# Attention bursts spaced one to a chunk, and a weight conversion with its own tiles, in a fused attention and cosine-FFN kernel

## The chip, the cores and the metric

The kernel runs on one core of one Trainium2 chip. The metric is the device time of one execution in microseconds (us). Three executions of the kernel before took 988.85, 989.06 and 987.37 us, so the median is 988.85 us. The profile was taken of a further execution, of 985.93 us.

## The reference, cut to what matters

```python
# batch 8, heads 8, sequence 576, head size 64; 4608 tokens, model size 512, hidden size 2048
scores = matmul(q, k.T) / 8
mask_local   = (0 <= i - j) & (i - j < 32)            # heads 0 to 3
mask_strided = (0 <= i - j) & (i % 32 == j % 32)      # heads 4 to 7
attn = softmax(where(mask, scores, -1e9))             # denominators + 1e-9
x    = matmul(attn, v)             # to 4608 x 512, heads side by side
h    = x @ w_in                    # 512 x 2048
out  = (h * cos(h)) @ w_out        # 2048 x 512
```

Everything is in 32-bit floats at the kernel's borders. Eight batches of 576 tokens make 4608 tokens.

## The kernel before, in words

**The feed-forward part.** Tokens are handled in 12 blocks of 384 (TB). For block j and for each of 16 slices f of the hidden size (128 rows each) there is one *chunk* (j, f). `hidden` makes h in one PSUM bank from 12 matmuls. The operands are split into a rounded part and a remainder: x_hi and x_lo, wi_h and wi_l, and three products of them are summed for each of four slices of the model size. Then h * cos(h) is made by a chain over two engines: ScalarE rounds h to a multiple of the period (line 377), VectorE subtracts it (378), ScalarE takes the sine shifted by a quarter (381), VectorE multiplies by h (384). Only after line 384 is the bank of h free; there are two such banks (`ps_h`, bufs=2). ScalarE then rounds the result to g_hi (387), and GpSimd makes the remainder g_lo (388). `outer` multiplies g by the slice of w_out with nine matmuls into three accumulators. `outer` runs three chunks behind `hidden` (LAG = 3).

**The attention part.** Each batch has ten *units*: four strided ones, then six local ones (two head pairs for each of three stretches of 192 tokens). A unit makes scores on TensorE, a softmax over VectorE, ScalarE and GpSimd, transposes on TensorE, products with v on TensorE, and a copy and a DMA of the result to a DRAM tensor xT. `load_x(j)` reads the four slices of a block back from xT: a DMA into x_raw, a cast to x_hi on VectorE (361) and a remainder x_lo on GpSimd (362).

**The three stages.** First, the 20 units of batches 0 and 1 run alone (0 to about 61 us). Second, blocks 0 and 1 run together: chunk (0, f), then chunk (1, f-1), while the weights of slice f are loaded and converted, and then three chunks of block 2. Third comes the steady loop: blocks 2 to 11, chunk by chunk, with the units of batches 2 to 7 put between the chunks in *bursts*. It numbers its chunks n from 3 to 159, where n = 16 (j - 2) + f. Burst k issues the transposes of unit k-2, the products of unit k-3 and the scores of unit k. At which chunk burst k is issued comes from linear interpolation between the pairs of KNOTS (chunk, burst), cut to whole chunks. In this loop TensorE's order is written out by hand (`in_turn`: each matmul after the one before it).

**The weights.** They come as 64-bit floats, seen as pairs of 32-bit words (low, top). `load_weight` takes one block of 128 x 512 numbers (512 KB): a DMA on SP's queue into the tile `raw`, of which the pool `cv` keeps two; on VectorE a shift of the low words (line 120) and an or with the sign of the top words (123); on ScalarE a scaling of the top words in place (128); on VectorE a last shift and or (129), whose result stands in the low words of the same tile; on ScalarE the cast to the rounded weights (133); on GpSimd the remainder (134). So a landing tile is in use until line 134 has read it. For each f, one such block of w_in and one of w_out are converted. The first operation of each (120) is ordered behind line 378 of the chunk two slices before (`after`, AHEAD = 2).

**What sets the order.** Each engine, and SP's queue of DMAs, works in the order of its instructions. Apart from TensorE in the steady loop, a scheduler chooses that order from the program's order and from its own estimate of the times. An operation that it expects to be ready early is moved forward, and blocks what is behind it if its input is late on the chip.

**Lines that the prediction names**: 118 (DMA of a weight block), 120, 123, 128, 129, 133, 134 (its conversion), 210 to 231 (softmax), 254 and 297 (scores), 264 and 313 (transposes), 273 and 327 (products), 279 and 281 (copy and store of a local unit), 360 to 362 (`load_x`), 371 to 388 (`hidden`), 395 (`outer`).

## Time and profile before

| what | value |
|---|---|
| median of three executions | 988.85 us |
| profiled execution: whole time | 985.93 us |
| profiled execution: span of the core's instructions | 984.1 us |
| granted TensorE clock, mean | 0.997 |
| TensorE (PE) busy | 954.8 us, 97% |
| VectorE (DVE), ScalarE (ACT), GpSimd (POOL) busy | 48%, 51%, 39% |
| bytes moved by DMA | 80.14 MB |

The engines are called PE, PEld (the loading of PE's weights, beside its matmuls), DVE, ACT, POOL and SP. A row of a timeline has the start in us from the span's start, the duration in us, the engine, the line, the operation, out<-in and the shape; in brackets the idle time before it and what ended it. "SPq" and "ACTq" are the instructions that issue DMAs. A row of groups has the count, the busy time, the mean in ns, and the idle time just before them. The row of a stretch has the stretch, its length, each engine's busy time with its number of instructions, the granted clock, the DMA engines' share and GB/s.

### The profile page before, as it was taken

The numbers are of one execution on the slowest core, as the hardware profiler recorded it, in microseconds if no ns is written. First come the engines' busy times: TensorE is split into PE (matmuls) and PEld (weight loads), VectorE is DVE, ScalarE is ACT, GpSimd is POOL, SyncE is SP. The second block draws the span as 40 slices with busy tenths as digits, with TensorE's granted clock in tenths as the row PEclk, the third lists the DMA queues.
The fourth block names the chain that finished last, engine by engine and source line by source line (L and its number), as shares of the span: only waits on it lengthen the run. The fifth ranks groups of instructions, "written<-read, shape, count | busy, mean of one in ns | idle before, by whom it ended". The sixth has DMA issues, their size and how long they took to land.

```text
span 984.1 us, 17763 instructions
## 1 busy us (share of the span) xinstructions
PE 954.8 (97%) x6890; PEld 833.9 (85%) x6890; DVE 467.9 (48%) x1005; ACT 499.6 (51%) x1043; POOL 384.4 (39%) x418
## 2 busy tenths in 40 slices
PE   9889899897999999999999999999999999999998
PEld 5678777786888888889888888888888888889997
DVE  6867777645454444444444444444444444222222
ACT  3665555555555545555445545555455544433433
POOL 2555544544344344334333343433333343232221
PEclk9999999999999999999999999999999999999999
DMA  8963333232332222112221332211221320100000
GB/s 247 296 216 108 108 111 124 66 108 73 104 87 91 68 87 79 43 51 75 69 59 43 110 85 75 75 51 54 90 60 35 111 60 14 46 15 1 33 1 32
DMA packets 48228, 80.14 MB, mean 81 GB/s; under 512 B 5904, under 2 KB 33296, under 8 KB 48144
## 3 DMA queue, kind: packets, MB, share of 16 engines
q1 hardware_dynamic: 38208, 69.35, 22.8%
q10 hardware_dynamic: 9936, 9.65, 2.8%
q8 instruction: 54, 0.88, 0.4%
q14 instruction: 30, 0.25, 0.1%
HBM read 60.11 MB, written 18.87 MB: 80 GB/s over the span
## 4 chain that ended last, share of the span: by engine, by line
PE 77%; DMA 2%; DVE 2%; ACT 2%; issue 1%; POOL 1%; POOLq 0%; DVEq 0%; ACTq 0%; SPq 0%
PE h L371 35%; PE acc L395 34%; PE acc L273 2%; PE acc L254 2%; DMA raw<-in_w_out 1%; PE acc L297 1%; PE acc L264 1%; PE acc L327 1%; PE acc L313 1%; DVE raw L120 1%; DVE raw L129 0%; ACT raw L128 0%; DVE r L378 0%; POOL g_lo L388 0%; DMA xT<-x_t 0%
## 5 line engine op out<-in xcount | busy, mean ns | idle before, releaser
L388 POOL TENSOR_TENSOR g_lo<-r,g_hi 128x384 fp32r<-128x384 f32 x192 | 198.6, 1034 | 401.1 <-issue 257.4
L371 PE MATMUL h<-x_hi,wi_h 128*128 128x384 f32 x768 | 267.1, 348 | 14.6 <-DVE r L384 14.6
L371 PE MATMUL h<-x_hi,wi_l 128*128 128x384 f32 x768 | 259.3, 338 | 0.0
L371 PE MATMUL h<-x_lo,wi_h 128*128 128x384 f32 x768 | 258.8, 337 | 0.0
L378 DVE SCALAR_TENSOR_TENSOR r<-r,h 128x384 f32<-128x384 int32 x192 | 106.2, 553 | 265.8 <-ACT r L377 247.3
L395 PE MATMUL acc<-wo_l,g_hi 128*128 128x512 f32 x576 | 227.4, 395 | 0.0
L395 PE MATMUL acc<-wo_h,g_lo 128*128 128x512 f32 x576 | 224.7, 395 | 0.0
L395 PE MATMUL acc<-wo_h,g_hi 128*128 128x512 f32 x576 | 224.0, 389 | 0.0
L371 PEld LDWEIGHTS h<-x_hi,wi_h 128*128 128x128 f32 x768 | 144.7, 188 | 31.5 <-DVE r L384 21.6
L381 ACT ACTIVATE r<-r,quarter 128x384 f32<-128x384 f32 x192 | 118.5, 617 | 91.1 <-DVE r L378 90.5
L371 PEld LDWEIGHTS h<-x_lo,wi_h 128*128 128x128 f32 x768 | 144.7, 188 | 5.0
L377 ACT ACTIVATE r<-h 128x384 int32<-128x384 f32 x192 | 93.4, 486 | 108.8 <-PE h L371 102.7
L384 DVE TENSOR_TENSOR r<-r,h 128x384 f32<-128x384 f32 x192 | 106.0, 552 | 81.8 <-ACT r L381 81.0
L371 PEld LDWEIGHTS h<-x_hi,wi_l 128*128 128x128 f32 x768 | 144.5, 188 | 0.3 <-POOL wi_l L134 0.3
L387 ACT CAST g_hi<-r 128x384 fp32r<-128x384 f32 x192 | 98.5, 513 | 83.5 <-DVE r L384 83.4
L395 PEld LDWEIGHTS acc<-wo_h,g_lo 128*128 128x128 f32 x576 | 108.0, 188 | 23.0
L395 PEld LDWEIGHTS acc<-wo_l,g_hi 128*128 128x128 f32 x576 | 108.0, 188 | 18.2
L395 PEld LDWEIGHTS acc<-wo_h,g_hi 128*128 128x128 f32 x576 | 108.2, 188 | 17.2
L362 POOL TENSOR_TENSOR x_lo<-x_raw,x_hi 128x384 fp32r<-128x384 f32 x48 | 50.0, 1042 | 107.1 <-DVE x_hi L361 86.8
L220 ACT ACTIVATE e_sb<-t_sb,shift 128x288 f32<-128x288 f32 (+1 forms) x60 | 32.9, 549 | 87.2 <-POOL t_sb L212 87.0
L361 DVE CAST x_hi<-x_raw 128x384 fp32r<-128x384 f32 x48 | 21.3, 445 | 53.0 <-DMA x_raw<-xT 50.7
L212 POOL TENSOR_TENSOR t_sb<-t_sb,mx 128x288 f32<-128x288 f32 (+1 forms) x60 | 41.8, 696 | 10.1 <-DVE mx L211 8.5
(66 smaller groups left out, 860.5 us busy)
## 6 DMA issues: line engine op xcount, KB each, us to landing
qk<-in_qkvs SPq DMA_DIRECT2D x32, 324.0 KB, 3.7
qk<-in_qkl SPq DMA_DIRECT2D x48, 208.0 KB, 2.7
x_raw<-xT SPq DMA_DIRECT2D x48, 192.0 KB, 2.4
out<-o SPq DMA_DIRECT2D x36, 256.0 KB, 2.1
raw<-in_w_in SPq DMA_DIRECT2D x16, 512.0 KB, 3.6
raw<-in_w_out SPq DMA_DIRECT2D x16, 512.0 KB, 3.7
v<-in_vl SPq DMA_DIRECT2D x48, 144.0 KB, 2.7
xT<-x_t ACTq DMA_DIRECT2D x16, 288.0 KB, 3.2
```

The costliest lines, as they stand in the source:

```text
L212: nc.gpsimd.tensor_tensor(out=t, in0=t, in1=mx[:, :n].unsqueeze(2).broadcast_to([P, n, w]), op=ALU.subtract)
L220: nc.scalar.activation(out=e, in_=t, func=AF.Silu, bias=shift1, scale=0.0625)
L361: nc.vector.tensor_copy(out=hi, in_=raw)
L362: nc.gpsimd.tensor_tensor(out=lo, in0=raw, in1=hi.bitcast(F32), op=ALU.subtract)
L371: mm = nc.tensor.matmul(h, w[:, f, c], x[c], start=(i == 0), stop=(i == len(ops) - 1))
L377: nc.scalar.activation(out=k, in_=h, func=AF.Copy, scale=1.0 / (2.0 * math.pi), bias=0.25)
L378: red = nc.vector.scalar_tensor_tensor(out=r, in0=k, scalar=-2.0 * math.pi, in1=h, op0=ALU.mult, op1=ALU.add)
L381: sin = nc.scalar.activation(out=r, in_=r, func=AF.Sin, bias=quarter)
L384: nc.vector.tensor_tensor(out=r, in0=r, in1=h, op=ALU.mult)
L387: nc.scalar.copy(out=g_hi, in_=r)
L388: nc.gpsimd.tensor_tensor(out=g_lo, in0=r, in1=g_hi.bitcast(F32), op=ALU.subtract)
L395: mm = nc.tensor.matmul(acc[t], g[:, ts], w[:, f], start=(f == 0 and i == 0), stop=(f == NFC - 1 and i == 2))
```

## The change

In the steady loop, the knots move: before, bursts 0 to 11 lay on chunks 3 to 12, and two chunks had two bursts (3 and 7); after, bursts 0 to 10 lie on chunks 3 to 13, one each. The knots behind them move one chunk later, and so does `load_x` of the next block, from f = 13 to f = 14.

In the conversion of the weights, the result is built in a tile of its own, `bits` (two of them), and only line 129 is left to read the landing tile last; there are three landing tiles. For w_out, the shift of the low words is done on ScalarE instead of VectorE (a copy with a scale and an offset, from unsigned words to whole numbers), and that conversion is no longer ordered behind `reduced`. For w_in, VectorE does the shift and the order stays.

In `load_x`, x_raw is no longer a tile of its own (there were two): the DMA lands in the x_lo tile (eight of them), and the remainder is made in place. The three constants for biases share one tile.

```diff
-KNOTS = ((3, 0), (12, 11), (28, 19), (60, 31), (76, 39), (124, 59), (140, 63))
+KNOTS = ((3, 0), (13, 10), (29, 19), (61, 31), (77, 39), (125, 59), (141, 63))
 UNIT_LAG = 2
-LOAD_AT = 13
+LOAD_AT = 14
...
-    xp = ctx.enter_context(tc.tile_pool(name="xp", bufs=2))
...
-    shift1, shift2, quarter = (const.tile([P, 1], F32, name=n) for n in ("shift1", "shift2", "quarter"))
+    biases = const.tile([P, 3], F32, name="biases")
+    shift1, shift2, quarter = (biases[:, n:n + 1] for n in range(3))
...
-    def load_weight(cv, src, hi, lo, after):
+    def load_weight(cv, src, hi, lo, after, scalar):
...
-        first = nc.vector.tensor_scalar(out=low, in0=low, scalar1=29, scalar2=None, op0=ALU.logical_shift_right)
-        if after is not None:
-            order(first, after, "weights no earlier than they are needed")
+        bits, scaled = cv.tile([P, 512], I32, name="bits", bufs=2), top.bitcast(F32)
+        if scalar:
+            nc.scalar.activation(
+                out=bits, in_=low.bitcast(U32), func=AF.Copy, scale=2.0 ** -29 * (1.0 - 2.0 ** -16),
+                bias=7.5 * 2.0 ** -16 - 0.5,
+            )
+        else:
+            first = nc.vector.tensor_scalar(out=bits, in0=low, scalar1=29, scalar2=None, op0=ALU.logical_shift_right)
+            if after is not None:
+                order(first, after, "weights no earlier than they are needed")
         nc.vector.scalar_tensor_tensor(
-            out=low, in0=top, scalar=-0x80000000, in1=low, op0=ALU.bitwise_and, op1=ALU.bitwise_or
+            out=bits, in0=top, scalar=-0x80000000, in1=bits, op0=ALU.bitwise_and, op1=ALU.bitwise_or
         )
-        nc.scalar.activation(out=top.bitcast(F32), in_=top.bitcast(F32), func=AF.Copy, scale=2.0 ** -112)
+        nc.scalar.activation(out=scaled, in_=scaled, func=AF.Copy, scale=2.0 ** -112)
         nc.vector.scalar_tensor_tensor(
-            out=low, in0=top, scalar=3, in1=low, op0=ALU.logical_shift_left, op1=ALU.bitwise_or
+            out=bits, in0=top, scalar=3, in1=bits, op0=ALU.logical_shift_left, op1=ALU.bitwise_or
         )
-        w = low.bitcast(F32)
+        w = bits.bitcast(F32)
...
-                wi_l[:, f].rearrange("p c n -> p (c n)"), after,
+                wi_l[:, f].rearrange("p c n -> p (c n)"), after, False,
             )
-            load_weight(cv, w_out.bitcast(I32)[f], wo_h[:, f], wo_l[:, f], after)
+            load_weight(cv, w_out.bitcast(I32)[f], wo_h[:, f], wo_l[:, f], after, True)
...
-            raw = xp.tile([P, TB], F32, name="x_raw")
             hi = xs.tile([P, TB], F32R, name="x_hi")
             lo = xs.tile([P, TB], F32R, name="x_lo")
+            raw = lo.bitcast(F32)
...
-        cv = loading.enter_context(tc.tile_pool(name="cv", bufs=2))
+        cv = loading.enter_context(tc.tile_pool(name="cv", bufs=3))
```

More of the change, by code (lines that the diff above doesn't have):

```diff
@@ L17 @@
 I32 = mybir.dt.int32
+U32 = mybir.dt.uint32
 AF = mybir.ActivationFunctionType
```

## The prediction

> **What bounds the kernel now.** I began with the busy time in four stretches: attention alone, the two blocks with their weights, the first bursts, and the rest.
>
> ```profile
> 0.00:50.00 50.00, 45.61 (x670) 30.19 (x672) 36.02 (x109) 24.14 (x59) 21.04 (x30) 1.00 0.86 272
> 61.02:215.05 154.03, 141.78 (x708) 122.77 (x709) 104.59 (x155) 86.31 (x162) 80.66 (x68) 1.00 0.35 114
> 215.05:251.40 36.35, 29.70 (x325) 26.01 (x325) 19.75 (x50) 21.93 (x48) 14.97 (x20) 0.91 0.30 94
> 251.40:972.20 720.80, 720.80 (x5066) 641.51 (x5066) 298.77 (x669) 357.43 (x755) 261.16 (x294) 1.00 0.20 59
> ```
>
> From 251 us on PE never stops: nothing there can be won but by less PE work. PE is idle for 12.25 us (154.03 - 141.78) in the second stage and for 6.65 us (36.35 - 29.70) in the first bursts. The waits of PE from 64 to 250 us name the causes:
>
> ```profile
> PE h L371 <- DVE r L384: 12.2, 13, 2.4
> PE acc L264 <- POOL e_sb L231: 3.6, 1, 3.6
> PE acc L313 <- POOL pn_s L231: 2.2, 1, 2.2
> ```
>
> PE waits 13 times for a bank of h that DVE has not yet read, and twice for a softmax. Why DVE is late, shows the timeline of one pair of slices (POOL, SP, DVE, ACT, PE, in order of time):
>
> ```profile
> 154.01 1.32 POOL L134 TENSOR_TENSOR wo_l<-raw,wo_h 128x512 fp32r<-128x512 f32 x1
> 155.35 0.33 SPq L118 DMA_DIRECT2D raw<-in_w_out  x1
> 159.03 1.22 DVE L120 TENSOR_SCALAR raw<-raw 128x512 int32<-128x512 int32 x1 [1.22 <-DMA raw<-in_w_out]
> 160.17 0.54 DVE L378 SCALAR_TENSOR_TENSOR r<-r,h 128x384 f32<-128x384 int32 x1
> ...
> 161.40 0.55 DVE L384 TENSOR_TENSOR r<-r,h 128x384 f32<-128x384 f32 x1
> 162.01 0.45 PE L371 MATMUL h<-x_hi,wi_h 128*128 128x384 f32 x1 [0.70 <-DVE r L384]
> ```
>
> POOL releases the landing tile at 155.33, SP issues the next block at once, and it lands 3.6 us later. DVE stands in front of line 120 for 1.22 us with line 378 behind it; ACT's sine, line 384 and PE follow late. SP's waits and the issues of one of the two matrices, from 64 to 195 us, show that this is the rule and not one case:
>
> ```profile
> SPq L118 <- POOL wi_l L134: 55.7, 13, 5.1
> SPq L118 <- POOL wo_l L134: 50.7, 13, 4.9
> ...
> L118 SPq DMA_DIRECT2D raw<-in_w_in x13: 327/328/333, 65.6 to 179.3; - x13
> ```
>
> All 26 transfers waited for POOL. Thirteen issues from 65.6 to 179.3 us are 12 periods of 9.47 us, one for a pair of chunks. What PE needs for a pair, shows the chain of waits where PE runs free:
>
> ```profile
> 200.45 2.10 PE h L371 x12
> 202.56 2.08 PE acc L395 x9
> ```
>
> 2 x (2.10 + 2.08) = 8.36 us. Over 12 periods the excess is 12 x 1.11 = 13.3 us: the 12.2 us of idle time, and about 0.1 us more for each restart (its first matmul takes 0.45 us).
>
> **Part 1, the landing tiles.** After the change a landing tile is free when line 129 ends, not when line 134 ends two operations later, and there are three. The groups from 64 to 195 us give the conversion's prices:
>
> ```profile
> L120 DVE TENSOR_SCALAR raw<-raw 128x512 int32<-128x512 int32 x26 | 23.1, 888 | 13.7 <-DMA raw<-in_w_out 8.3 <-DMA raw<-in_w_in 5.3
> L123 DVE SCALAR_TENSOR_TENSOR raw<-raw 128x512 int32<-128x512 int32 x26 | 24.8, 953 | 0.6
> L129 DVE SCALAR_TENSOR_TENSOR raw<-raw 128x512 int32<-128x512 int32 x27 | 19.7, 730 | 11.8 <-ACT raw L128 11.4
> L128 ACT ACTIVATE raw<-raw 128x512 f32<-128x512 f32 x26 | 17.4, 670 | 28.0 <-DVE raw L123 24.2 <-POOL wi_l L134 3.2
> L381 ACT ACTIVATE r<-r,quarter 128x384 f32<-128x384 f32 x28 | 17.2, 616 | 11.1 <-DVE r L378 11.1
> L384 DVE TENSOR_TENSOR r<-r,h 128x384 f32<-128x384 f32 x28 | 15.4, 549 | 4.7 <-ACT r L381 4.4
> ```
>
> The least, median and most of the first two, over the same stretch:
>
> ```profile
> L120 DVE TENSOR_SCALAR raw<-raw x26: 416/900/1551, 69.6 to 187.7; 128x512 int32<-128x512 int32 x26
> L123 DVE SCALAR_TENSOR_TENSOR raw<-raw x26: 680/694/1823, 70.4 to 188.2; 128x512 int32<-128x512 int32 x26
> ```
>
> With three tiles and two blocks per 8.36 us, a tile may be held 12.5 us. It is held for the transfer (3.6 us) and for lines 120 to 129 (0.888 + 0.953 + 0.670 + 0.730 = 3.2 us, with the waits between them some 4 us): 5 us of room, so DVE's 13.7 us of waiting for DMA should go nearly whole. What is late next is DVE or ACT themselves. DVE's work for a pair is now 2 x (0.888 + 0.953 + 0.730 + 0.549 + 0.549) = 7.34 us, line 378 taken like line 384. Without one line 120 it is 6.45 us, 77% of 8.36. ACT has two each of lines 128, 381, 377, 133 and 387. By lines 128 and 381 as bounds that is between 10 x 0.616 = 6.2 and 10 x 0.670 = 6.7 us.
>
> The new shift on ACT isn't in the trace. Line 128, the same shape and engine, bounds it above with 0.670 us; below stands the least that DVE takes for it, 0.416 us. I take 0.670. ACT then has 6.9 to 7.4 us of 8.36, the fullest of the three beside PE. Its shift waits for the landing, and lines 377 and 381 stand behind it on ACT's queue, with DVE and PE behind those. No engine has to exceed PE, but orders aren't perfect: of the 13.3 us I take 80% as won, 10.7 us; the bounds are 0 and 13.3.
>
> A rule of the Trainium skill speaks against part of this. Row: line 120 takes 0.888 us in the mean and 0.416 us at least, line 123 up to 1.823 us where its median is 0.694 us. "SBUF — State Buffer", section "Who interferes with whom", says that DVE and GpSimd share one port pair that is locked for a whole instruction, and that a DVE instruction with two SBUF inputs contends for it too. By it the wait that line 120 sheds moves to the next two-input line, 123. DVE would save 0.42 us per pair instead of 0.89 us; were DVE the pace, the stage would win 13 x 0.47 = 6 us less.
>
> **Part 2, the bursts.** Chunks 3 and 7 had two bursts each, so a unit scored in burst k had one chunk instead of two before its transposes in burst k+2. Both softmax waits of PE are just these. After the change every transpose of the first ten bursts lies two chunks behind its scores. The second case:
>
> ```profile
> 236.95 0.45 DVE L210 TENSOR_TENSOR t_sb<-acc,ml 128x288 f32<-128x288 f32 x1
> ...
> 242.48 0.36 DVE L361 CAST x_hi<-x_raw 128x384 fp32r<-128x384 f32 x1 [0.85 <-DMA x_raw<-xT]
> 242.92 0.99 POOL L362 TENSOR_TENSOR x_lo<-x_raw,x_hi 128x384 fp32r<-128x384 f32 x1 [3.53 <-DVE x_hi L361]
> ...
> 244.82 0.67 POOL L231 TENSOR_TENSOR e_sb<-e_sb,z 128x288 f32<-128x288 f32 x1
> 245.54 0.88 PE L264 MATMUL acc<-ident,e_sb 128*96 128x128 f32 x3 [3.55 <-POOL e_sb L231]
> 247.68 3.72 PE h L371 x12
> ...
> 254.94 2.31 PE h L371 x12
> ...
> 260.80 2.30 PE h L371 x12
> ```
>
> The unit's softmax began at 236.95 and was ready at 245.49 us, 8.5 us later; POOL had stood 3.53 us in front of a forwarded x_lo, and the softmax's last step waited behind it. One burst in a chunk makes a chunk of 5.86 us (260.80 - 254.94); two are 11.7 us, so both waits go: 3.6 + 2.2 = 5.8 us. After the long wait the matmuls of h took 3.72 instead of 2.31 us, in the stretch whose clock stands at 0.91; that goes as well: 1.4 us. In return two bursts no longer share a chunk. A change from chunk to burst and back costs about 0.2 us (h takes 2.30 instead of 2.10 us): 0.4 us for two. The later knots only shift bursts that PE does anyway: 0.
>
> **Part 3, the hand-over of block 3.** Its last slice now depends on the products in chunk 13 instead of 11, while the block still starts at chunk 16. The path before:
>
> ```profile
> 271.89 0.32 ACT L279 COPY x_l<-acc 128x192 f32<-128x192 f32 x1
> ...
> 279.33 1.20 POOL L362 TENSOR_TENSOR x_lo<-x_raw,x_hi 128x384 fp32r<-128x384 f32 x1 [2.74 <-DVE x_hi L361]
> ...
> 298.33 2.28 PE h L371 x12
> ```
>
> From the copy (271.89) to the end of x_lo (280.53) it takes 8.6 us, and the block began 17.8 us after that. Chunks 12 and 13 with a burst each are 10 to 11.7 us less room: 6 us are left. I take 0. If the room failed, DVE's cast would stand waiting in front of lines 378 and 384, and POOL's x_lo in front of g_lo and the softmaxes.
>
> **Part 4, load_x without its own tile.** In the steady loop the x_lo tiles of the block before last are long free, so four transfers can be issued instead of two: 0. For block 2 the transfers must now wait until chunk (0, 15) has read its x_lo, behind which stores and the steady loop's loads stand on SP's queue. Until block 2 begins PE has two h and three acc groups, 2 x 2.10 + 3 x 2.08 = 10.4 us; needed are a transfer (3.7 us under load), a cast and four x_lo and two g_lo of 1.0 us, about 10 us, the last of them not before the end of h. I take 0; it costs 2 us at most. The biases are 0.
>
> **Part 5, attention alone.** Its transfers hold the DMA engines at a share of 0.86.
>
> ```profile
> raw<-in_w_in SPq DMA_DIRECT2D x3, 512.0 KB, 5.7
> x_raw<-xT SPq DMA_DIRECT2D x8, 192.0 KB, 3.7
> ...
> DVE x_hi L361 <- DMA x_raw<-xT: 4.3, 5, 2.1
> ```
>
> Three blocks of w_in come in the first 60 us, and as many of w_out. With three tiles, and w_out not ordered behind `reduced`, up to three more can, with their conversions: 1.57 MB at 272 GB/s are 5.8 us if all of it is on the path. On the other side, loads of x with more tiles can shorten DVE's longest wait there, 2.1 us. Bounds -2.1 and +5.8; I take +1, as a late start also finds slices already converted.
>
> **Sum**, against the profiled execution of 985.93 us: -10.7 -5.8 -1.4 +0.4 +1.0 = -16.5, so 969.4 us. That execution lies 2.9 us below the median of 988.85, which puts the median after at 972.3 us.
>
> **The rivals.** *The conversion stays the pace* (DVE's long lines, ACT's order): 9.47 us per pair remain, only the bursts are won: 985.93 - 5.8 - 1.4 + 0.4 + 1.0 = 980.1, a median of 983. For it: DVE at 77% and ACT above 80%; against: 13.7 us of DVE's waiting end by DMA. *The extra weights pay in full in stage one*: 969.4 + 4.8, a median of 977. For it the DMA share, against it that SP issues weights last. *Block 3 comes late*: the 5.8 us come back at chunk 16, a median of 978; against it the 6 us of room. *Slower: ACT becomes the pace of the second stage.* The w_out shift, in nobody's order, stands early on ACT's queue and waits for its landing, with lines 377 and 381 behind it. If ACT keeps its idle times of today, each pair is 0.67 us longer, 13 x 0.67 = 8.7 us, and the unordered conversions fill stage one (5.8 us): 985.93 + 8.7 + 5.8 - 7.2 + 0.4 = 993.6, a median of 996.5. It decides from about 10.0 us per pair, where 13 x 0.53 us eat up the bursts. For it: ACT's 24.2 us of waiting for line 123. Against: with three tiles the landing lies a pair ahead. That the bursts stay doubled is excluded by the knots.
>
> **Chances.** Forecast 0.60, its own range 965 to 979. Conversion stays the pace 0.18, stage one pays 0.08, block 3 late 0.06, slower 0.08. Within 0.2% (2 us, what a measurement can tell) only part of the second and fourth lie: 0.05. So faster 0.87, same 0.05, slower 0.08. All stalls won, with the best of part 5: 985.93 - 13.3 - 7.2 - 2.1 + 0.4 = 963.7; the low end is 963. The high end, 984, takes in the first three rivals.
>
> **What would show it.** Right: issues of w_in about 8.4 us apart in the second stage, no idle DVE in front of line 120, PE without waits between 217 and 250 us, the hidden groups at 2.1 to 2.3 us. Wrong: periods above 9 us with waits of PE on line 384 that lead back to ACT's shift or to line 123; the first h later than 61 us by more than 3; a wait of PE for x_lo near chunk 16.

## The result, and the profile after

The changed kernel takes 973.01 us in the median of four executions (969.51 to 974.36). The kernel before, measured beside it, takes 988.95 us in the median of four (987.37 to 990.37). The ratio is 0.9837, with a 95% interval of 0.9807 to 0.9866. The profiled execution took 974.17 us, with a span of 972.4 us, so it is 11.76 us shorter than the profiled one of before (985.93 us).

All lines of the code lie 2 to 10 further down after the change: the DMA of a weight block is L120; the first shift L125 (ACT, for w_out) or L130 (DVE, for w_in); the or's L133 and L139; the scaling L138; the cast L143; the remainder L144; `load_x` L370 to L372; `hidden` L381 to L398; `outer` L405. The stretches of the kernel after, in the columns explained above, cut at its own borders (the third group of 12 matmuls of h begins at 67.49 us, chunk n = 3 at 207.91 us):

```profile
0.00:50.00 50.00, 45.74 (x549) 29.06 (x550) 32.42 (x92) 21.66 (x51) 17.87 (x25) 0.86 0.79 250
67.49:207.91 140.42, 140.42 (x732) 125.87 (x732) 81.60 (x142) 93.59 (x177) 78.75 (x67) 0.99 0.36 121
207.91:251.40 43.49, 43.15 (x402) 37.04 (x398) 25.68 (x63) 26.99 (x59) 19.27 (x24) 1.00 0.30 94
251.40:960.00 708.60, 707.26 (x4966) 626.38 (x4967) 289.87 (x656) 350.62 (x742) 255.86 (x290) 1.00 0.20 59
```

In the second stage PE no longer stops at all (140.42 of 140.42 us), and in the first bursts it stops for 0.34 us (43.49 - 43.15), where it was 12.25 and 6.65 us. What is left of PE's waits from 64 to 190 us is one row, before that stretch of full work:

```profile
PE h L381 <- DVE r L394: 2.7, 1, 2.7
```

The weights run ahead now. SP's waits and its issues of one matrix, 64 to 195 us, kernel after:

```profile
SPq L120 <- DVE bits L139: 58.0, 24, 5.3
SPq L120 <- DMA raw<-in_w_out: 26.5, 10, 2.9
SPq L370 <- PE h L381: 19.3, 1, 19.3
...
L120 SPq DMA_DIRECT2D raw<-in_w_out x13: 327/328/333, 68.1 to 164.9; - x13
```

Twelve periods now take 96.8 us, 8.07 us each, where they took 9.47. That is less than the 8.36 us of PE's pair of chunks, so blocks come faster than PE uses them up. The conversion's groups of that stretch, kernel after:

```profile
L133 DVE SCALAR_TENSOR_TENSOR bits<-raw,bits 128x512 int32<-128x512 int32 x28 | 19.9, 745 | 1.2 <-ACT bits L125 1.2
L138 ACT ACTIVATE raw<-raw 128x512 f32<-128x512 f32 x28 | 18.0, 681 | 6.8 <-DVE bits L133 6.8
L139 DVE SCALAR_TENSOR_TENSOR bits<-raw,bits 128x512 int32<-128x512 int32 x28 | 19.1, 713 | 0.1
L130 DVE TENSOR_SCALAR bits<-raw 128x512 int32<-128x512 int32 x13 | 8.7, 672 | 1.5 <-POOL wo_l L144 1.3 <-POOL wi_l L144 0.3
L125 ACT ACTIVATE bits<-raw 128x512 int32<-128x512 uint32 x13 | 8.6, 664 | 0.3 <-POOL wi_l L144 0.2
```

DVE's 13.7 us of waiting for a landing are gone, and DVE does not wait long for anything else there.

**Where the 11.76 us of the two profiled executions lie.** The start of chunk n = 3 splits each span into what the weights and attention alone set, and what the steady loop sets. The rows of both kernels:

```profile
217.49 0.45 PE L371 MATMUL h<-x_hi,wi_h 128*128 128x384 f32 x1
```

```profile
207.91 0.44 PE L381 MATMUL h<-x_hi,wi_h 128*128 128x384 f32 x1
```

Up to there 9.6 us are won; the prediction had 9.7 (10.7 less the 1.0 of attention alone). From there to the end it is 984.14 - 217.49 = 766.7 against 972.38 - 207.91 = 764.5 us: only 2.2 us are won where the prediction had 6.8. And inside the first part the two terms are far from the forecast: the third group of h begins 6.5 us later than before (61.02 to 67.49), and the way from it to chunk n = 3 is 16.0 us shorter (156.5 to 140.4). So the total came out as forecast, and three of its parts did not: the steady loop, the second stage and attention alone. The experiments take them apart.

The timeline of PE in the kernel after, and its stretches, show where attention alone became longer (columns as above, the clock third from the end):

```profile
21.31 0.30 PE L200 MATMUL h<-ml,ident 128*128 128x288 bf16 x1
23.77 1.23 PE L264 MATMUL h<-qk 64*64 64x96 f32 x12 [2.16 <-DMA qk<-in_qkl]
```

```profile
22.00:24.00 2.00, 0.23 (x4) 0.24 (x6) 2.00 (x7) 1.32 (x4) 0.40 (x1) 0.79 0.93 307
24.00:30.00 6.00, 6.00 (x49) 3.91 (x49) 4.52 (x9) 2.38 (x6) 2.52 (x3) 0.50 0.60 184
30.00:37.00 7.00, 7.00 (x77) 4.78 (x74) 3.73 (x14) 2.58 (x7) 2.55 (x3) 0.51 0.87 306
```

PE waits 2.16 us for a transfer of q and k, and then works for 13 us at a granted clock of 0.50 (half speed). The kernel before has no such place; its rows of the same two stretches:

```profile
24.00:30.00 6.00, 4.93 (x94) 3.77 (x95) 5.37 (x14) 4.65 (x13) 2.46 (x3) 1.00 0.95 342
30.00:37.00 7.00, 6.69 (x119) 4.69 (x119) 6.41 (x22) 3.17 (x8) 5.76 (x8) 1.00 0.88 271
```

### The profile page after: what moved, and what is told of

It is laid out like the page before. It is cut to its first block, busy times and chain, and to the rows that moved or that the text cites. A ratio compares the mean times of both kernels' runs of the same rounds, so it can differ in the third digit from the quotient of the medians.

```text
span 972.4 us, 17730 instructions
## 1 busy us (share of the span) xinstructions
PE 959.6 (99%) x6890; PEld 836.8 (86%) x6890; DVE 445.6 (46%) x989; ACT 506.5 (52%) x1059; POOL 383.2 (39%) x418
## 4 chain that ended last, share of the span: by engine, by line
PE 91%; DMA 4%; ACT 1%; issue 1%; POOL 1%; DVE 1%; SPq 0%; ACTq 0%; POOLq 0%; DVEq 0%
PE h L381 41%; PE acc L405 40%; PE acc L283 2%; PE acc L264 2%; PE acc L307 2%; PE acc L337 1%; PE acc L274 1%; DMA x_lo<-xT 1%; PE acc L323 1%; DMA xT<-x_t 1%; PE acc L478 1%; DMA raw<-in_w_out 1%; DMA qk<-in_qkl 1%; DMA xT<-x_l 0%; DMA v<-in_vl 0%
## 5 line engine op out<-in xcount | busy, mean ns | idle before, releaser
L398 POOL TENSOR_TENSOR g_lo<-r,g_hi 128x384 fp32r<-128x384 f32 x192 | 198.6, 1034 | 404.2 <-issue 257.7
L381 PE MATMUL h<-x_hi,wi_h 128*128 128x384 f32 x768 | 265.7, 346 | 2.7 <-DVE r L394 2.7
L381 PE MATMUL h<-x_hi,wi_l 128*128 128x384 f32 x768 | 259.4, 338 | 0.0
L381 PE MATMUL h<-x_lo,wi_h 128*128 128x384 f32 x768 | 258.0, 336 | 0.0
L405 PE MATMUL acc<-wo_l,g_hi 128*128 128x512 f32 x576 | 226.9, 394 | 0.0
L405 PE MATMUL acc<-wo_h,g_hi 128*128 128x512 f32 x576 | 226.9, 394 | 0.0
L405 PE MATMUL acc<-wo_h,g_lo 128*128 128x512 f32 x576 | 226.1, 395 | 0.0
L391 ACT ACTIVATE r<-r,biases 128x384 f32<-128x384 f32 x192 | 118.3, 616 | 84.5 <-DVE r L388 82.1
L381 PEld LDWEIGHTS h<-x_hi,wi_h 128*128 128x128 f32 x768 | 144.4, 188 | 13.9 <-DVE r L394 3.2
L381 PEld LDWEIGHTS h<-x_lo,wi_h 128*128 128x128 f32 x768 | 144.7, 188 | 5.9
L381 PEld LDWEIGHTS h<-x_hi,wi_l 128*128 128x128 f32 x768 | 144.5, 188 | 0.0
L405 PEld LDWEIGHTS acc<-wo_h,g_lo 128*128 128x128 f32 x576 | 107.7, 187 | 26.3
L405 PEld LDWEIGHTS acc<-wo_l,g_hi 128*128 128x128 f32 x576 | 107.8, 187 | 18.0
L405 PEld LDWEIGHTS acc<-wo_h,g_hi 128*128 128x128 f32 x576 | 107.7, 187 | 18.0
L372 POOL TENSOR_TENSOR x_lo<-x_lo,x_hi 128x384 fp32r<-128x384 f32 x48 | 50.3, 1049 | 117.7 <-DVE x_hi L371 100.4
L230 ACT ACTIVATE e_sb<-t_sb,biases 128x288 f32<-128x288 f32 (+1 forms) x60 | 32.9, 549 | 92.1 <-POOL t_sb L222 92.0
L371 DVE CAST x_hi<-x_lo 128x384 fp32r<-128x384 f32 x48 | 21.0, 440 | 66.1 <-DMA x_lo<-xT 62.8
```

The lines of the kernel that those rows point to most:

```text
L230: nc.scalar.activation(out=e, in_=t, func=AF.Silu, bias=shift1, scale=0.0625)
L371: nc.vector.tensor_copy(out=hi, in_=raw)
L372: nc.gpsimd.tensor_tensor(out=lo, in0=raw, in1=hi.bitcast(F32), op=ALU.subtract)
L381: mm = nc.tensor.matmul(h, w[:, f, c], x[c], start=(i == 0), stop=(i == len(ops) - 1))
L391: sin = nc.scalar.activation(out=r, in_=r, func=AF.Sin, bias=quarter)
L398: nc.gpsimd.tensor_tensor(out=g_lo, in0=r, in1=g_hi.bitcast(F32), op=ALU.subtract)
```

## The experiments

All of them in one table, so that the texts can refer to it. "n = 3" is the start of the first matmul of h in that chunk, "steady" the span's end less that start. "Chunk" is the mean time of a chunk in the last stretch without bursts: the starts of the first matmul of h in the 19th-last and in the last of the 192 chunks, divided by 18. "Third" is the start of the third group of h. "Ratio" is to the kernel before as it ran beside that kernel (medians 988.95, 988.73, 988.43 and 987.85 us for after, e1 to e4, e5 to e8, e9 to e12); third, n = 3, steady and chunk are of one profiled execution each.

```
run                     median us  ratio, 95%               third   n = 3   steady  chunk
before (profile)        988.95     1                        61.02   217.49  766.7   4.1867
after  (profile)        973.01     0.9837 [0.9807, 0.9866]  67.49   207.91  764.5   4.2000
e1  bursts only         979.25     0.9917 [0.9884, 0.9949]  61.62   217.10  760.6   4.1867
e2  after, old bursts   980.09     0.9929 [0.9907, 0.9951]  66.17   210.68  771.3   4.2000
e3  w_out ordered       973.84     0.9862 [0.9831, 0.9894]  63.42   206.15  763.8   4.2000
e4  constants merged    989.76     1.0022 [0.9996, 1.0048]  61.05   217.58  770.9   4.2000
e5  more filler         976.44     0.9881 [0.9861, 0.9901]  70.02   210.73  763.3   4.2000
e6  two landing tiles   971.31     0.9844 [0.9817, 0.9871]  60.87   204.24  763.8   4.2000
e7  address 0           969.96     0.9816 [0.9796, 0.9837]  63.88   203.97  763.3   4.1933
e8  address 64          968.62     0.9815 [0.9785, 0.9845]  61.85   202.47  764.2   4.2067
e9  after, again        971.28     0.9844 [0.9819, 0.9869]  64.28   206.06  763.2   4.2000
e10 two tiles, 64       972.77     0.9845 [0.9823, 0.9868]  64.59   207.26  763.7   4.2067
e11 e10, w_out ordered  972.58     0.9845 [0.9818, 0.9872]  63.52   206.36  764.4   4.2067
e12 own result tile     978.16     0.9908 [0.9881, 0.9935]  58.63   207.90  768.3   4.1866
```

### The bursts alone, and all but the bursts (e1, e2)

e1 is the kernel before with the two lines of the first hunk; e2 is the kernel after with these two lines as they were.

```diff
-KNOTS = ((3, 0), (12, 11), (28, 19), (60, 31), (76, 39), (124, 59), (140, 63))
+KNOTS = ((3, 0), (13, 10), (29, 19), (61, 31), (77, 39), (125, 59), (141, 63))
-LOAD_AT = 13
+LOAD_AT = 14
```

> The kernel before with the new knots and the new LOAD_AT alone. Theory (the bursts win the two softmax waits of 5.8 us and 1.4 us of slow clock, and pay 0.4 us for two more changes): 6 to 7 us below the kernel before, a median near 982, and no wait of PE on a softmax between 215 and 252 us; stage two unchanged with 9.47 us per pair. Rival (the profiles of the two kernels differ by only 2 to 3 us behind the first steady chunk, so the bursts win no more than that and something new is lost): 2 to 3 us below, a median near 986.

> The kernel after with the old knots and the old LOAD_AT, so the changes of the weights and of load_x alone. Theory: it gives back the 6 to 7 us of the bursts, a median near 979.5, with PE's waits on the softmax back at chunks 4 and 7 of the loop. Rival (bursts are worth 2 to 3 us): near 975.5.

The steady part of e1 is 6.1 us shorter than that of before (766.7 to 760.6), and that of after is 6.8 us shorter than that of e2 (771.3 to 764.5). The forecast was 6.8 us. In the medians e1 is 9.5 us below the kernel before (988.73 to 979.25), more than the 6 to 7 us expected, and after is 7.1 us below e2. In e2 the two waits of PE from 190 to 255 us are back, with the prices that they had:

```profile
PE acc L274 <- POOL e_sb L241: 3.6, 1, 3.6
PE acc L323 <- POOL pn_s L241: 2.2, 1, 2.2
```

So the size of the bursts' term is right. Most of the steady loop's missing microseconds come from elsewhere: e2 has all but the bursts, and its steady part is 4.6 us longer than that of before. But the waits on a softmax are not gone for good. In the profile of after two shorter ones follow behind the first bursts, 1.6 us together, with POOL standing in front of an x_lo before each:

```profile
248.84 1.01 POOL L372 TENSOR_TENSOR x_lo<-x_lo,x_hi 128x384 fp32r<-128x384 f32 x1 [3.57 <-DVE x_hi L371]
...
252.13 0.53 PE L274 MATMUL acc<-ident,e_sb 128*96 128x128 f32 x3 [1.01 <-POOL e_sb L241]
...
267.93 1.01 POOL L372 TENSOR_TENSOR x_lo<-x_lo,x_hi 128x384 fp32r<-128x384 f32 x1 [6.02 <-PE h L381]
...
270.62 0.53 PE L274 MATMUL acc<-ident,e_sb 128*96 128x128 f32 x3 [0.60 <-POOL e_sb L241]
```

e1 has one such wait (0.8 us at 261.06), and the second profile of the kernel after (e9, below) has none.

### One part of the conversion: the result's own tile (e12)

The kernel before, with the result in a tile of its own; two landing tiles, every shift on DVE and all orders stay.

```diff
-        first = nc.vector.tensor_scalar(out=low, in0=low, scalar1=29, ...)
+        bits = cv.tile([P, 512], I32, name="bits", bufs=2)
+        first = nc.vector.tensor_scalar(out=bits, in0=low, scalar1=29, ...)
...
-            out=low, in0=top, scalar=-0x80000000, in1=low, ...
+            out=bits, in0=top, scalar=-0x80000000, in1=bits, ...
...
-            out=low, in0=top, scalar=3, in1=low, ...
+            out=bits, in0=top, scalar=3, in1=bits, ...
...
-        w = low.bitcast(F32)
+        w = bits.bitcast(F32)
```

> The kernel before with one part of the change: the result of the conversion is built in a tile of its own, so that the landing tile is free after its last or on DVE. Two landing tiles, every shift on DVE, both orders, the old bursts, the constants at their old addresses. Theory A (early release alone carries the gain of the second stage): no wait of PE on DVE between 64 and 190 us but one or two at its head, 16 f later issues 8.4 us apart or less, 986 - 13 to 986 - 10 = 973 to 976 us profiled, 976 to 979 in the median. Theory B (DVE needs one of its two shifts moved to ACT, or the third tile): periods of 9 us or more for a pair of chunks, waits of PE of 6 us or more there, a median of 983 or more.

The median is 978.16 us (976.72 to 981.09), as theory A has it; the profiled execution, 977.96 us, is 2 us above its range. Chunk n = 3 begins at 207.90 us, as early as in the first profile of the kernel after, whose third group begins 8.9 us later (67.49 against 58.63). SP issues the blocks of w_in 8.39 us apart (71.1 to 163.4 us, 11 periods), which is PE's own pace. PE's waits from 64 to 190 us (lines are one further than before):

```profile
PE h L372 <- DVE r L385: 3.5, 1, 3.5
PE h L372 <- DVE x_hi L362: 1.5, 1, 1.5
```

Both are single waits; the 12 regular ones are gone. And DVE's first shift, which stayed on DVE twice in a pair, became short by itself; its group in e12, 64 to 195 us:

```profile
L121 DVE TENSOR_SCALAR bits<-raw 128x512 int32<-128x512 int32 x26 | 11.9, 489 | 3.8 <-DMA raw<-in_w_out 2.1 <-DMA raw<-in_w_in 1.7
```

489 ns in the mean, where line 120 took 888. Whether the dense tile as its destination makes it shorter or the different moment, no run tells apart. For the time it means: the result's own tile takes the regular waits away, and neither the shift on ACT nor the third tile is needed for that. The tile does two things: it releases the landing tile earlier, and it goes with shorter lines on DVE, by 0.40 us (888 to 489 ns) and 0.21 us (953 for line 123 to 747 for L124 here) a block. As each of two landing tiles is held for one period, these 0.6 us could at most, as an estimate, take 0.6 of the 1.11 us that a period was too long; the earlier release is needed for the rest, and no run separates the two. Whether the shift on ACT and the third tile add something is not separated either. From its third group to n = 3 PE is still idle for 6.7 us in e12, in single waits, and e6, which has the shift on ACT and two landing tiles, begins n = 3 3.7 us earlier (204.24); two profiles of one kernel differ by 1.9 us there (after and e9).

### The third landing tile, and the order of w_out (e6, e3)

e6 is the kernel after with two landing tiles. e3 is the kernel after with the order behind `reduced` given back to w_out's conversion.

```diff
-        cv = loading.enter_context(tc.tile_pool(name="cv", bufs=3))
+        cv = loading.enter_context(tc.tile_pool(name="cv", bufs=2))
```

```diff
-            nc.scalar.activation(
+            first = nc.scalar.activation(
...
-            if after is not None:
-                order(first, after, "weights no earlier than they are needed")
+        if after is not None:
+            order(first, after, "weights no earlier than they are needed")
```

> The kernel after with two landing tiles instead of three (the separate bits tiles, the shift on ScalarE and the free order of w_out stay). Theory (the early release by line 139 and not the third tile is what takes the landing off DVE's path: a tile is held some 7.6 us of the 8.4 us that two tiles allow): stage two nearly without waits, 0 to 3 us of them, the attention stage 1 to 2 us shorter for one block less, and the time within 2 us of the kernel after. Rival (the third tile carries the gain): waits of PE on line 394 of 6 us and more in stage two, and 4 us or more above the kernel after.

> The kernel after with the conversion of w_out ordered behind reduced again, as that of w_in is (its first operation still on ScalarE). Theory (the blocks of w_out that are loaded and converted during the attention stage make it longer, by 6.5 us up to the third group of h, which began at 61.0 us before and at 67.5 us after): the third group begins 3 to 6 us earlier than after, at 62 to 64 us, stage two stays without waits, and the time is 3 to 5 us below the kernel after, near 969. Rival (the transfers come anyway with three landing tiles, and PE's slow clock between 20 and 40 us is what costs, set off by DVE's work at 15 to 25 us, which is slices 0 and 1): no change, near 973, with the clock at 0.5 to 0.8 between 20 and 40 us again.

e6 takes 971.31 us (969.84 to 974.88), e3 973.84 us (971.70 to 974.15): neither can be told from the kernel after. In e6 PE waits 2.9 us in all between 64 and 190 us, never more than 1.1 us at once, so that two tiles are enough. With two tiles SP waits more for landings than with three, and less for DVE (e6, 64 to 190 us):

```profile
SPq L120 <- DVE bits L139: 49.0, 24, 4.1
SPq L120 <- DMA raw<-in_w_out: 38.0, 9, 4.7
```

e3's profile has the third group 4.1 us earlier than after's. e11 repeats that edit on another base, below, and e9 shows that the kernel after has such a difference between two of its own profiles, so it isn't shown to be the order's.

### The constants alone: where the steady loop lost its time (e4)

The kernel before with the three constants in one tile, and nothing else.

```diff
-    shift1, shift2, quarter = (const.tile([P, 1], F32, name=n) for n in ("shift1", "shift2", "quarter"))
+    biases = const.tile([P, 3], F32, name="biases")
+    shift1, shift2, quarter = (biases[:, n:n + 1] for n in range(3))
```

> The kernel before with its three constants in one tile, and nothing else: all tiles made after them lie 64 bytes lower. Theory (the address of the operands sets the pitch of the matmuls of outer, which was 227, 232 and 236 ns in turn before and 233 ns each after): the pitch becomes 233 ns each, 15 ns more per chunk, and the time 3 us more, near 992. Rival (the pitch was that of another chip or clock, or has to do with the changed x and weight tiles): 227, 232 and 236 ns as before, and the time of the kernel before.

Both traces have the same operations in the same order on every engine. What differs is where the tiles behind the constants lie: 64 bytes lower, so that the weights, x and r begin at 32 modulo 128 bytes in the compiled program and not at 96; g stays where it was. The first matmul of h, in the 19th-last and the last chunk, kernel before and then e4 (line 372 there):

```profile
894.58 0.33 PE L371 MATMUL h<-x_hi,wi_h 128*128 128x384 f32 x1
...
969.93 0.33 PE L371 MATMUL h<-x_hi,wi_h 128*128 128x384 f32 x1
```

```profile
898.54 0.34 PE L372 MATMUL h<-x_hi,wi_h 128*128 128x384 f32 x1
...
974.14 0.34 PE L372 MATMUL h<-x_hi,wi_h 128*128 128x384 f32 x1
```

18 chunks take 75.36 us before and 75.60 us in e4, each one 13.3 ns more. PE does not wait in either stretch. The table has 4.1867 in the three kernels with the constants apart (before, e1, e12) and 4.2000 in all with the constants merged in this way. Between the starts of `outer`'s matmuls, from 500 to 700 us, lie 227.2, 232.2 and 235.8 ns in the kernel before (from wo_h with g_hi to wo_l, to g_lo, and to the next), and 233.3 to 233.4 ns for each kind in e4. The sum of three is 4.8 ns longer; three times that for a chunk is 14 ns.

Over the 157 chunks of the steady loop 13.3 ns are 2.1 us, and the end behind the last chunk's start is 0.17 us longer: 2.3 us. e4's steady part is 4.2 us longer than before's, that of e2 3.0 us longer than that of e12, and that of e9 (the kernel after again) 2.6 us longer than that of e1. So the addresses are shown as the cause of 2.3 us, while the rest, 0.3 to 1.9 us, differs from pair to pair. In e4 the granted clock accounts for most of it. Behind the first softmax wait (2.2 us in both profiles) it stays at 1.00 in the kernel before and falls in e4:

```profile
220.04:223.45 3.41, 1.91 (x9) 1.21 (x7) 2.31 (x7) 3.05 (x7) 0.45 (x2) 1.00 0.02 8
223.45:226.86 3.41, 2.71 (x35) 2.48 (x36) 2.19 (x6) 1.16 (x3) 2.62 (x4) 1.00 0.11 19
```

```profile
221.59:225.00 3.41, 1.23 (x16) 0.62 (x16) 3.01 (x9) 2.31 (x6) 0.81 (x2) 1.00 0.00 0
225.00:228.41 3.41, 3.41 (x30) 3.31 (x25) 0.99 (x2) 1.11 (x3) 2.34 (x3) 0.50 0.22 62
```

3.41 us at 0.50 are 1.7 us lost, beside a rest of 1.9 us. e2 and e12 both have such a stretch there (0.51 and 0.50, from 218.6 and 215.7 us), e9 and e1 both have none, and in these two pairs the rest is only 0.7 and 0.3 us, which stays open. In the whole time e4 gives 1.0022, and its interval holds 1: a loss of this size is seen in the traces and not for certain in the medians.

### Other addresses (e7, e8)

The kernel after, with the constants in the spare end of another tile, which begins the tiles at 0 modulo 128, or in a tile that is longer by 13 columns, which begins them at 64.

```diff
-    ms = const.tile([P, GB], BF16, name="ms")
+    ms_t = const.tile([P, GB + 6], BF16, name="ms")
+    ms = ms_t[:, :GB]
...
-    biases = const.tile([P, 3], F32, name="biases")
+    biases = ms_t[:, GB:].bitcast(F32)
```

```diff
-    biases = const.tile([P, 3], F32, name="biases")
+    biases = const.tile([P, 16], F32, name="biases")
```

> The kernel after with its three constants in the unused end of the mask tile, so that the tiles behind lie 32 bytes lower, at multiples of 128 bytes (the weights for h and outer, x, r). Theory (the address sets the pitch of the matmuls): the pitch of the matmuls of outer, 233 ns each in the kernel after, changes by more than 1 ns on some kind of them, and that of h may; each ns on the 9 matmuls of outer is 1.7 us over 192 chunks. If a start at a multiple of 64 bytes is the cheaper one, pitches fall below 231 ns and the time falls by 3 us or more. Rival (only which of two neighbouring operands lies where matters, and a start at an odd multiple of 32 is no worse): 231 to 234 ns, and the time within 2 us of the kernel after.

> The kernel after with 32 bytes more in the tile of the constants, so that the same tiles lie 64 bytes above a multiple of 128. Theory: as for the start at a multiple of 128, and by the difference to it one sees whether 64 bytes are the unit (the same pitches as there) or 128. Rival: 231 to 234 ns, and the time within 2 us of the kernel after.

The chunk is 4.1933 us at 0 and 4.2067 us at 64: each start has its own value, and none is below the 4.1867 of the kernel before. The steady parts (763.3 and 764.2) are those of the kernel after. Nevertheless the medians are the lowest of all, 969.96 and 968.62 us. That comes from before n = 3, which begins at 203.97 and 202.47 us. e10 has e8's addresses and begins it at 207.26 us, with a median of 972.77: the early start of e8 isn't shown to be the addresses'. What the addresses do is settled for the chunk and nothing else.

### Attention alone and the clock (e9, e5)

e9 is the kernel after, unedited. e5 is the kernel after with more of the filling matmuls (`warm`) that keep PE busy there:

```diff
-BUSY = (10, 6, 5, 3, 2, 2, 2) + 8 * (1,)
+BUSY = (10, 6, 5, 3, 3, 3, 3) + 8 * (3,)
```

> The changed kernel itself once more, nothing edited. Its earlier profile had the clock at 0.50 from 24 to 37 us and the third group of h at 67.5 us; its four executions lay at 969.5, 971.9, 974.2 and 974.4 us. Theory A (whether the clock falls in attention alone changes from execution to execution): the executions again spread over 969 to 975 us, and a profile without the fall has the third group at 61 to 64 us and a time of 969 to 971 us. Theory B (it is fixed by the order of the instructions): the profile again shows 0.50 near 24 to 37 us, the third group at 67 to 68 us, and the executions gather at 973 to 975 us.

> The kernel after with more of the filling matmuls that keep PE busy in the attention stage (three after each of the steps 3 to 13 instead of two or one; their results are not used). Theory (PE's pause at 20 to 24 us, in which DVE is fully busy with early weights, halves its clock until 38 us, and that makes the attention stage longer): the clock stays at 1.0 from 20 to 40 us, the third group of h begins at 64 to 65.5 us instead of 67.5, and the time is 2 to 3 us below the kernel after. Rival (DVE and the transfers set that stage, the clock only follows): clock 1.0, but the third group near 67 us and no change of time.

The same kernel, in e9's profile, in the stretches shown above for after:

```profile
22.00:24.00 2.00, 1.46 (x17) 0.82 (x14) 2.00 (x7) 1.59 (x6) 0.94 (x1) 1.00 1.07 331
24.00:30.00 6.00, 5.50 (x72) 3.97 (x73) 5.43 (x15) 3.18 (x7) 2.94 (x4) 0.72 0.90 288
30.00:37.00 7.00, 6.74 (x118) 4.66 (x114) 5.52 (x18) 3.24 (x9) 4.25 (x6) 1.00 0.95 297
```

Here PE works for 1.46 of the 2 us that were nearly empty in the other profile; the clock falls for a shorter time (0.50 from 24.7 to 28.1 us), and the third group begins at 64.28 and not at 67.49 us. The whole execution took 971.05 us, 3.1 less. So the length of attention alone changes from execution to execution of one kernel, and the clock changes with it: theory A in the main. e8, which differs from the kernel after in addresses alone and issues the same seven blocks of weights in this stage, shows the stage without any fall. The whole stage in after, e9 and e8, in turn:

```profile
0.00:67.40 67.40, 60.05 (x758) 40.90 (x758) 46.55 (x127) 32.38 (x77) 28.15 (x37) 0.90 0.75 238
0.00:64.20 64.20, 55.61 (x758) 38.19 (x758) 46.77 (x127) 32.39 (x77) 28.47 (x37) 0.97 0.79 250
0.00:61.80 61.80, 54.16 (x758) 37.39 (x758) 44.96 (x127) 32.56 (x77) 28.47 (x37) 1.00 0.81 260
```

At 1.00 throughout, the third group begins at 61.85 us, 0.8 us later than before. e6, too, has 1.00 throughout and begins it at 60.87 us. The clock isn't all: e12 has it at 0.50 from 24.5 to 31.3 us and yet begins its third group first of all, at 58.63 us.

The nine executions of the kernel after lie between 969.51 and 974.36 us, with a median of 971.85. The five executions of e9 spread less than theory A had them (971.05 to 973.27), and the fall isn't gone in its profile: there two pauses of 0.77 and 1.04 us (at 21.1 and 23.5 us) stand before it. The kernel before idles 1.07 of the 6 us from 24 us on, and keeps 1.00. What decides, when a pause is short, is narrowed in the last section and not settled.

More filling does not help. e5 is slower, 976.44 us (974.44 to 977.45), and its clock falls too, behind a pause that the filler did not cover:

```profile
32.00:36.00 4.00, 1.89 (x26) 1.02 (x24) 3.35 (x13) 1.70 (x5) 2.74 (x4) 0.93 1.01 348
36.00:42.00 6.00, 5.36 (x47) 3.45 (x49) 1.82 (x6) 1.74 (x4) 1.73 (x2) 0.50 0.74 218
```

The filler stands between the units' matmuls in PE's order, and a pause that comes from a late transfer is not filled by it. So more filling is no remedy here, and of the two theories neither held: the clock fell all the same.

### Parts put together (e10, e11)

e10 is the kernel after with e8's longer tile and two landing tiles (e6); e11 has e3's order as well. The diffs are those shown.

> The changed kernel with two landing tiles in place of three and with the constants' tile 64 bytes longer, so that x, the weights and r start at 64 modulo 128. One alone gave 971.3 us with the third group of h at 60.9 us, the other 968.6 us with 61.9 us. Theory A (both act by the same thing, a stage one without the fall of the clock): no sum of the two, 968 to 971 us. Theory B (two separate savings, fewer early transfers and addresses): 966 to 967.5 us. The steady part, from the chunk n = 3 to the end, should be 763 to 765 us by both.

> As the run before it, and the first operation of a block of w_out is ordered behind line 378's counterpart of two slices before, as that of w_in is (this puts nothing early on ACT's queue in attention alone). Theory A (the w_out conversions that nobody orders cost attention alone some 2 to 4 us): 1 to 4 us below the run before it, 965 to 968 us. Theory B (they lie beside other work): within 1 us of it.

972.77 us (970.17 to 973.43) and 972.58 us (968.70 to 974.50): above both theories' ranges for e10, so nothing of what e6 and e8 seemed to have, alone, is left when they are joined, and the order of w_out is worth nothing that can be told (theory B of e11). e10's profile has its slow clock from 35 to 50 us (0.69, and 0.64 from 40 us), e11's from 35 to 40 us (0.70). The steady parts, 763.7 and 764.4 us, are as expected. No version is shown to beat the changed kernel: from e6 to e11, and with after itself, the steady parts lie within 1.3 us (763.2 to 764.5), while chunk n = 3 begins anywhere from 202.5 to 207.9 us, in two profiles of one kernel too (207.91 and 206.06).

## Why the prediction was right, and which terms were not

**Part 1, the landing tiles: right in its mechanism, too cautious in size.** The stall of the second stage was the hold on the landing tile. e12 shows that the result's own tile by itself takes the regular waits away, by the earlier release and, which the prediction did not have, by shorter lines on DVE. The 80% should have been all of it: in after, PE does not wait from 67.49 us on until chunk n = 3. The shift on ACT, estimated at 0.670 us, takes 0.664 us; SP's periods, estimated at 8.4 us, are 8.07 us, because the weights run ahead and no longer follow PE.

The Trainium skill, "SBUF — State Buffer", section "Who interferes with whom", was weighed with the prediction that DVE's shed wait would move to the two-input line behind it. The trace shows no such move: that line went from 953 ns (L123) to 745 ns (L133), beside a GpSimd that was at work for 78.75 of 140.42 us. Its result goes to another tile now, too, so this is no test of the page's rule itself.

**Part 5, attention alone: the mis-sized term.** Forecast was +1.0, with 5.8 us as the upper bound, from the bytes of up to three more blocks. The first profile has +6.5 us, the second of the same kernel +3.3 us, and the bytes are not it: e8 issues as many blocks, and has +0.8 us where the clock stays at 1.00. SP's issues before 62 us, kernel after:

```profile
L120 SPq DMA_DIRECT2D raw<-in_w_in x4: 354/407/432, 7.2 to 32.6; - x4
L120 SPq DMA_DIRECT2D raw<-in_w_out x3: 328/424/434, 7.6 to 28.2; - x3
```

Seven blocks against six: 0.52 MB, 1.9 us at the 272 GB/s of the prediction's row. What I had left out is the clock, so that a wait of PE in this stage is paid twice: 2.16 us for q and k, and then 13 us in which PE is busy throughout at a clock of 0.50. That the clock makes the difference is argued from the profiles set side by side; the one run that was to keep the clock up by design, e5, did not keep it up. A first h that is late by more than 3 us was among the prediction's signs of being wrong; the total survived it, because the way from there to n = 3 was shorter by 16.0 and not by 10.7 us. Part of it is that a later start finds more ready, which the prediction said; the runs don't divide it further. Both terms together were forecast at -9.7 and came out at -9.6 us, and at -11.4 us in e9: two errors that cancelled, which is luck.

**Part 2, the bursts: right in the main.** Forecast -6.8 us, measured -6.1 (e1 against before) and -6.8 us (after against e2, whose profile has one more stretch of half clock than that of before). The clock of the first bursts went from 0.91 to 1.00, and the two waits there are gone; of the two shorter ones behind them, 1.6 us in after's profile, the prediction knew nothing.

**Part 3, block 3: right at the hand-over.** PE is idle for 0.34 us in all from 207.91 to 251.40 us, and there is no wait of PE for x_lo near chunk 16. But POOL's x_lo in front of the softmaxes, which the prediction named as the danger and put at 0, stands before both of the shorter waits (1.6 us).

**Part 4: right in `load_x`, wrong in the constants.** SP does stand waiting for PE to have read an x_lo, 19.3 us in one piece (L370, above), and PE does not wait for it. But "the biases are 0" is the step that failed. They cost no operation, and yet each chunk is 13.3 ns longer, through the addresses: 2.3 us of the steady part, and by the 35 chunks before it some 0.5 us more, as an estimate from the same 13.3 ns. The steady loop's 2.2 us in place of 6.8 are then 6.1 from the bursts (e1), less 2.3 for the addresses, less 1.6 for the two waits behind the first bursts.

**The sum.** Against its own base the forecast was 969.4 us profiled; the profiled execution was 974.17 us, 4.8 us above. The median, 972.3 us forecast and 973.01 us measured, agrees better because the profiled execution of before lay 2.9 us under its median and the profiled one of after lies 1.2 us over its own. Of the closeness, then, some 4 us is luck: the prediction's way from one profiled execution to a median was its weakest step, since attention alone differs by some microseconds between executions. e9's profile, 971.05 us, is 1.7 us above the forecast of 969.4.

**The rivals.** That the conversion stays the pace: no, periods are 8.07 us. That the extra weights pay in full in attention alone: the place was right, the cause was not (one more block and not three, and with the clock at 1.00 it costs 0.8 us). That block 3 comes late: no. That ACT becomes the pace: its shift waited 0.3 us in all, and giving w_out its order back (e3, e11) changes nothing.

## What to carry to other kernels

Ask of a double buffer how long each tile is *held*: here a result tile of its own, which lets go of it earlier, took away the regular waits without the third buffer and the other engine that were added with it. A profile of one execution is a base for differences only up to what that stage itself varies by; look for stretches where the clock falls, since a wait of 2.16 us stood here before 13 us at half clock. And an edit that changes no instruction can still move every tile behind it: compare the pitch of the same matmuls in both traces before a missing microsecond is looked for in waits.

## What the runs showed of the hardware that I had not expected

**Matmuls of one shape have a pitch that depends on where the operands begin.** With wo at 96, 32, 0 and 64 modulo 128 bytes, and g at 96 throughout, the three kinds of `outer`'s matmuls (128x512) start 227.2/232.2/235.8, 233.3/233.3/233.4, 234.5/231.9/235.8 and 232.0/233.8/233.4 ns apart (500 to 700 us, means over 81 to 123 pairs for a kind). x and r moved with wo, so it isn't shown which of the tiles matters. A chunk is 4.1867, 4.2000, 4.1933 and 4.2067 us in turn, the same in every run at one address, within 0.1 ns.

**The granted clock fell to 0.50 after pauses of PE of some 2 us, for 3.4 to 13.7 us.** After: 2.16 us idle at 21.6 us, then 0.50 from 23.2 to 36.9 us. In e9 two shorter pauses at the same place led to 0.50 from 24.7 to 28.1 us. The Trainium skill, "TensorE: Matmul & The Clock Gate", section "What's actually happening", has the half clock come after an idle window of about 3.4 us that runs freely, so that the moment differs from run to run. The traces agree: the falls of one profile begin whole multiples of 3.413 us apart, to within 0.01 us (there are four each in e2, e4 and e12), and every fall lasts one, two, three or four times that. But a window need not be idle throughout. Before each of the 24 falls up to 950 us, in the 14 profiles, PE was still busy for up to 0.66 of the last 3.41 us, for 0.55 or less in 23 of them; in after it was 1.81 us, in e4, shown above, 1.23. The kernel before kept its clock after a stretch with 1.91 us (shown beside it). So one wait of 2.2 us cost no clock there and 1.7 us in e4, by where the beat cut it. A sharp limit isn't shown: with 0.46 to 0.66 of a stretch busy, the clock fell in some cases and held in others.
